# Attention and soft mixture of experts on one core: logits summed in PSUM, late scaling spread over three engines, full durations for the first loads, and the loop's buffers laid out by last use

## The chip, the core and the metric

One core of a Trainium2 chip runs the whole program. A core has five engines with a queue each: TensorE (PE; its weight loads are shown as PEld), VectorE (DVE), ScalarE (ACT), GpSimd (POOL) and SyncE (SP, which only issues transfers here). They run side by side and wait for each other by semaphores. The metric is the device time of one execution in microseconds (us), lower is better.

## The reference, cut to what matters

```python
scores = q @ k.T / 8                       # 8 batches x 8 heads, 576 tokens, head size 64
thresh = max(scores, -1) - tau             # keep only what is near the row's maximum
attn   = exp(where(scores >= thresh, scores, -1e9) - max(scores, -1))
attn  /= sum(attn, -1) + 1e-9
x      = (attn @ v), heads side by side    # [4608, 512]

logits = x @ phi                           # 32 slots
d      = softmax(logits, axis=0)           # over the 4608 tokens, one per slot
slots  = d.T @ x                           # [32, 512], 4 slots for each of 8 experts
slots  = relu(slots @ w1[e]) @ w2[e]       # 512 -> 1024 -> 512
out    = softmax(logits, axis=1) @ slots   # [4608, 512]
```

All of it is fp32. The dispatch weights `d` need a maximum over all tokens, so the kernel keeps a running maximum per batch and rescales what it has summed so far.

## The kernel before

The 64 heads are worked through as 32 pairs, `pair(p)`, four to a batch. A pair has nine row blocks of 128 queries (the ninth holds the 64 left of both heads). For each block PE multiplies q and k (L517, the ninth L522), DVE copies the scores out of PSUM with their maximum (L531, "max"), ACT takes the exponential (L544), POOL works out the threshold (L547), and DVE masks and sums the row (L551, "mask"). PE then transposes the result (L441 through the helper `ptr`), ACT copies it to SBUF (L446, `pTa`, `pTb`, `pTl`), and PE multiplies with v (L621). A further transpose, a scaling by the row sums on POOL (L636) and a transpose back (L641) give `x` and `xT`. In the last pair no later step can carry the row sums, so POOL scales the nine 128x576 blocks themselves (L565), with the reciprocals worked out on POOL (L558) and DVE (L561).

After each batch's fourth pair `dispatch(b)` runs, woven into the next pair: the logits of the batch as four products, one for each pair of heads, side by side in four column groups of PE (L700); a copy (ACT, L446, `l`); ten transposes (L712); a sum over the four products (DVE L717, L719); a copy for the left-over tokens (POOL L722); a transpose back (L441) and the maximum (DVE L732, L735); the factor `f` (ACT L737); a transpose of the maximum (`M`), the difference (DVE L744, L748) and its exponential (ACT L746, L750); and the weighted sums `csum` and `acc` (PE L770, L775; DVE L783). After the last batch `scale()` (L655 to L661) and `slot_in()` (L671, L674) make the slots' inputs `siT`, and the experts follow (L934 `h`, L968 `so`), then the combine. The combine's softmax (`csoft`, L805 to L815) is done in pieces by DVE and ACT.

**What sets the order.** `Order.plan` schedules the operations of the loop before the program is written: each has a duration, what it reads and writes, and a priority from `TABLE`; buffers are handed out as they come free. `Order.run` writes the program in the order of the planned starts. Every engine then works strictly in that order. PSUM is four regions, `ps0` to `ps3`. Where PE would idle at the start and at the end, transposes of the identity are put in (L433, "fillers"); 38 of them may stand behind the last AV product.

**Weights.** 46 of the 64 weight units (512 KB each) are loaded before the experts start: 26 into slots of their own (`w`), and 20 (`host`) into memory that the loop's buffers give back. Before, those buffers lie in five levels ordered by hand, and a host load waits until all levels that it lies in are done with. The 18 other units go into `w` slots as the experts' first layer frees them. All transfers are issued by SP in order.

Of the kernel before, what the change touches and what calls it, by code (L numbers as in the profile page):

```python
# [1108 lines left out]
```

## Time and profile before

| | us |
|---|---|
| median of 3 runs | 565.8 (565.67 to 566.19) |
| the profiled execution | 567.0 |
| its span, first to last instruction | 565.2 |
| PE busy | 536.4 (95%) |
| DVE busy | 476.1 (84%) |
| ACT busy | 458.2 (81%) |
| POOL busy | 257.9 (46%) |
| granted TensorE clock, mean | 0.985 of full |

Times in the rows below are counted from the span's start. A row of the timeline gives start, duration, engine, line, operation, what is written and read, how many instructions were joined, and in brackets the idle time ahead of it and what ended it. Instructions on one engine overlap by their pipelines, so the distance between starts, not the duration, is what one costs its engine.

### The profile page before, as it was taken

The page shows a single profiled execution, that of the slowest core. Times are in us where ns is not written, and L with a number is a line of the kernel's source. Part 1 is how long each engine was busy: PE and PEld are TensorE (multiplying, and loading weights), DVE is VectorE, ACT ScalarE, POOL GpSimd, SP SyncE. Part 2 cuts the span into 40 slices and gives each one's busy share as a digit, 9 for nine tenths or more (in the row PEclk, how much of TensorE's full clock was granted, in tenths as well). Part 3 has the DMA queues.
Part 4 walks back from the last instruction along what each step waited for, and adds up shares of the span by engine and source line. Part 5 has one row for each costly group of instructions (what it writes and reads, how often), then busy time and mean ns, then how long its engine had stood idle before and what let it go on. Part 6 is the DMA issues. An engine that isn't in the chain of part 4 may idle for free. (4 is left out here: it accounts for less than half of the span.)

```text
span 565.2 us, 17532 instructions
## 1 busy us (share of the span) xinstructions
PE 536.4 (95%) x6652; PEld 341.4 (60%) x6652; DVE 476.1 (84%) x1342; ACT 458.2 (81%) x784; POOL 257.9 (46%) x489
## 2 busy tenths in 40 slices
PE   8799999999999999999999999999999998899990
PEld 7566665666566666666666656666666565544470
DVE  5899998999999999998999899999999899322192
ACT  3699998999889999999899989998999889411171
POOL 1555553455345544554455545555555347311030
PEclk9799999999999999999999999999999999999996
DMA  7355555465446544432333333333333312899488
GB/s 170 70 160 164 163 161 154 121 188 177 102 127 178 167 132 140 102 94 52 81 88 89 88 89 87 88 89 87 89 87 88 88 63 54 319 404 409 194 357 313
DMA packets 31988, 82.99 MB, mean 147 GB/s; under 512 B 4640, under 2 KB 12832, under 8 KB 31904
## 3 DMA queue, kind: packets, MB, share of 16 engines
q1 hardware_dynamic: 31904, 81.87, 48.3%
q8 instruction: 53, 0.87, 0.7%
q14 instruction: 31, 0.25, 0.1%
HBM read 72.42 MB, written 9.44 MB: 145 GB/s over the span
## 5 line engine op out<-in xcount | busy, mean ns | idle before, releaser
L531 DVE TENSOR_SCALAR_CACHE_REDUCE ss<-ps 128x576 f32<-128x576 f32 x288 | 209.2, 749 | 23.4 <-ACT l L446 8.1
L547 POOL TENSOR_SCALAR thr<-nmx,pabs 128x1 f32<-128x1 f32 x288 | 130.0, 453 | 177.7 <-DVE ss L531 165.8
L551 DVE SCALAR_TENSOR_TENSOR p<-ss,thr,p 128x576 f32<-128x576 f32 x256 | 205.2, 823 | 3.8 <-POOL thr L547 2.7
L544 ACT ACTIVATE p<-ss,nmx 128x576 f32<-128x576 f32 x256 | 190.4, 781 | 13.0 <-DVE ss L531 13.0
L517 PE MATMUL ps<-k,q 64*128 64x288 f32 x1024 | 165.6, 430 | 3.9 <-POOL k L497 1.8
L441 PEld LDWEIGHTS ps<-ident,p 64*128 64x128 f32 x2304 | 92.9, 140 | 29.5 <-DVE p L551 7.0
L441 PE MATMUL ps<-ident,p 64*128 64x64 f32 x2304 | 105.2, 226 | 3.9 <-DVE ss L531 1.9
L517 PEld LDWEIGHTS ps<-k,q 64*128 64x128 f32 x1024 | 84.9, 190 | 36.1 <-ACT pTb L446 8.8
L446 ACT COPY pTb<-ps 128x1024 f32<-128x1024 f32 (+1 forms) x95 | 83.7, 881 | 2.6 <-PE ps L441 1.4
L621 PE MATMUL ps<-pTb,vv 128*64 128x320 f32 x512 | 76.0, 439 | 2.1 <-ACT pTa L446 1.8
L446 ACT COPY pTa<-ps 128x1024 f32<-128x1024 f32 x64 | 65.7, 1026 | 2.3 <-PE ps L441 2.1
L621 PE MATMUL ps<-pTa,vv 128*64 128x256 f32 x512 | 62.3, 385 | 1.5 <-DVE ss L531 0.8
L621 PEld LDWEIGHTS ps<-pTb,vv 128*64 128x64 f32 x512 | 34.1, 136 | 31.6 <-ACT pTa L446 3.1
L621 PEld LDWEIGHTS ps<-pTa,vv 128*64 128x64 f32 x512 | 33.9, 136 | 27.7 <-DVE ss L531 11.8
L621 PE MATMUL ps<-pTl,vv 128*64 128x256 f32 (+1 forms) x256 | 41.9, 406 | 0.0
L446 ACT COPY xT<-ps 128x256 f32<-128x256 f32 (+1 forms) x63 | 25.2, 400 | 13.5 <-PE ps L621 13.5
L446 ACT COPY pTl<-ps 128x256 f32<-128x256 f32 x64 | 23.8, 372 | 13.1 <-PE ps L441 12.3
L636 POOL TENSOR_TENSOR x<-x,ri 128x512 f32<-128x512 f32 x31 | 33.1, 1069 | 1.6 <-ACT x L446 1.5
L558 POOL TENSOR_SCALAR ri<-r 128x1 f32<-128x1 f32 (+1 forms) x36 | 20.0, 555 | 23.2 <-DVE pL L551 21.4
L565 POOL TENSOR_SCALAR pL<-pL,ri 128x576 f32<-128x576 f32 x32 | 26.5, 830 | 8.4 <-DVE ri L561 5.7
L899 POOL TENSOR_TENSOR c<-lall,crow 128x512 f32<-128x512 f32 x9 | 9.3, 1043 | 39.9 <-PE ct L433 39.9
L497 POOL TENSOR_SCALAR k<-k,flag 128x576 f32<-128x576 f32 x31 | 23.8, 769 | 7.0 <-DMA k<-in_kT 6.4
(134 smaller groups left out, 564.8 us busy)
## 6 DMA issues: line engine op xcount, KB each, us to landing
w<-in_w SPq DMA_DIRECT2D x44, 512.0 KB, 6.6
q<-in_qT SPq DMA_DIRECT2D x62, 288.0 KB, 4.3
vv<-in_vt SPq DMA_DIRECT2D x32, 320.0 KB, 4.0
host<-in_w SPq DMA_DIRECT2D x20, 512.0 KB, 6.4
k<-in_kT SPq DMA_DIRECT2D x62, 144.0 KB, 4.5
out<-w SPq DMA_DIRECT2D x8, 512.0 KB, 3.3
out<-host SPq DMA_DIRECT2D x8, 512.0 KB, 6.1
out<-host SPq DMA_DIRECT2D x4, 256.0 KB, 4.7
```

Of the source, the lines that this page charges most:

```text
L441: nc.tensor.transpose(out=s[:, g, c:c + 64], in_=ins[g], identity=ident[rows[g], rows[g]], tile_position=(64 * g, 0))
L446: G.add("ACT", 51 + 0.833 * n, nom, lambda: nc.scalar.copy(*io()), r, w)
L497: sc = lambda e, kc=kc: lambda: e.tensor_scalar(out=kt.t[:, kc], in0=kt.t[:, kc], scalar1=flag8, **one)
L517: nc.tensor.matmul(s.t[:, g, 0:HS], qt.t[rows[g], h, c * 128:(c + 1) * 128], kt.t[rows[g], h * HS:(h + 1) * HS], start=True, stop=True, ti ...
L531: dve(674, t + OFF['mx'], [s], [ss, nmx], lambda s=s, ss=ss, nmx=nmx: nc.vector.tensor_scalar(out=ss.t.rearrange("p (a k) -> p a k", a=2), ...
L544: G.add("ACT", 668 if away else 630, t + OFF['ex'], lambda sv=sv, nmx=nmx, view=view, away=away: nc.scalar.activation(view().rearrange("p ...
L547: pool(250, t + OFF['th'], lambda nmx=nmx, thr=thr, away=away: nc.gpsimd.tensor_scalar(out=thr.t, in0=nmx.t, scalar1=1.0 if away else -1.0 ...
L551: fn=lambda sv=sv, thr=thr, view=view, i=i, away=away: nc.vector.scalar_tensor_tensor(out=view().rearrange("p (a k) -> p a k", a=2), in0=sv(),
L558: pool(292, t + OFF['ri'], lambda e=e: nc.gpsimd.tensor_scalar(out=ri.t[:, e], in0=r.t[:, e], scalar1=1e-9, scalar2=1.0, op0=ALU.add, op1= ...
L565: pool(725, t + OFF['sc'], lambda k=k, view=view_: nc.gpsimd.tensor_scalar(out=view(), in0=view(), scalar1=ri.t[:, k:k + 1], **one), [ri[c ...
L621: nc.tensor.matmul(lone(w)[h * 64:(h + 1) * 64, 0:n], vv.t[:, v0:v0 + 64], p0, start=(kb == 0), stop=(kb == 4), tile_position=(0, h * 64), ...
L636: G.add("POOL", 1040, u + 6.8, own="new", r=[ri[0]], w=[x[j]], fn=lambda: nc.gpsimd.tensor_tensor(out=wide(), in0=wide(), in1=ri.t[:, 0:8] ...
```

## The change

1. **Logits.** The four products of a batch are summed in PSUM, in one tile of 192 columns: the 128-token chunk c goes to column group c (128 columns), the left-over tokens to 64 more columns. That is 32 products in place of 8. DVE takes the negated maximum straight from PSUM, ACT the exponential (`dT`) and a copy (`l4`), 192 columns each; two transposes of each and three copies give `d`, `lmain`, `lleft`. L712, L717, L719, L722, L744, L748 and the loop's transposes of `lall`, `ll` and `M` go. `xl` is now one batch's own with its upper half zero, so each batch adds its left-over tokens (two batches together before).
2. **Late scaling.** In the last pair, block 6 is scaled by DVE and block 7 by ACT, the other seven by POOL; both steps of the reciprocals are DVE's.
3. **First loads.** The planned durations of the transfers of the first three pairs are raised; the order table is new throughout. The order of loads on SP changes.
4. **Memory.** Each loop buffer has a pool of its own; they lie in the order of their planned last use, and a host load waits only for the buffers that it lies in and those released ahead of them.
5. The combine's DVE steps that stood in the last pair stand in the one before; `st4` is made later, on POOL; `siT` lies in the memory of `phi`.

```diff
-        -69.29, -40.08, -54.39, -166.86, 33.12, -19.81, -19.80, -168.20, -0.40, -236.51, -236.95, -153.88, 373.52, -143.51,
+        -281.55, -274.51, -289.04, -324.15, -256.85, -229.96, -223.08, -437.64, -189.50, -529.88, -365.53, -419.93, 528.97, -434.38,
...
+LATE_DVE = (6,)
+LATE_ACT = (7,)
...
-            G.add("SP", 1340, t0 - 18 + hs[0], keys, w=[kt[h] for h in hs])
+            G.add("SP", 1340 if p else 700, t0 - 18 + hs[0], keys, w=[kt[h] for h in hs])
...
-                G.add("SP", 620, t0 - 18 + hs[0], lambda g=g, a=hs[0], z=hs[-1] + 1: nc.sync.dma_start(
+                G.add("SP", (625 if p == 0 else 1250) if p < 3 else 800, t0 - 18 + hs[0], lambda g=g, a=hs[0], z=hs[-1] + 1: nc.sync.dma_start(
...
-        G.add("SP", 450, t0 - 12, lambda: nc.sync.dma_start(vv.t, vt[b, j]), w=[vv], after=vload[-1:])
+        G.add("SP", 1400 if p < 3 else 800, t0 - 12, lambda: nc.sync.dma_start(vv.t, vt[b, j]), w=[vv], after=vload[-1:])
...
+                    if k in LATE_DVE:
+                        dve(740, t + OFF['sc'], [ri[c]], [dst_], lambda f=f: f(nc.vector))
+                    elif k in LATE_ACT:
+                        G.add("ACT", 650, t + OFF['sc'], lambda k=k, view=view_: nc.scalar.activation(
+                            view(), view(), AF.Copy, scale=ri.t[:, k:k + 1]), [ri[c]], [dst_])
+                    else:
+                        pool(725, t + OFF['sc'], lambda f=f: f(nc.gpsimd), [ri[c]], [dst_])
...
+            for o, q in ((slice(0, 128), lambda c: slice(c * 128, c * 128 + 128)), (slice(128, 192), lambda c: slice(SM, S))):
                 for k in range(HP):
-                    nc.tensor.matmul(
-                        lone(w)[k * 32:(k + 1) * 32, 0:n], phi_sb[:, k, :], xT[k].t[:, q],
-                        start=True, stop=True, tile_position=(0, 32 * k))
...
+                    for c in range(4):
+                        nc.tensor.matmul(
+                            lone(wl)[c * 32:(c + 1) * 32, o], phi_sb[:, k, :], xT[k].t[:, q(c)], start=(k == 0),
+                            stop=(k == HP - 1), tile_position=(0, 32 * c), skip_group_check=True)
...
+        dve(269, u + 1.3, [wl], [M["own"]] if b else [new["run"]], lambda: nc.vector.tensor_reduce(
+            out=M.t[:, 0:1] if b else new.t[:, 1:2], in_=lone(wl)[:, 0:192], axis=AX.X, op=ALU.max, negate=True))
...
+        G.add("ACT", 250, u + 1.6, lambda: nc.scalar.activation(
+            dT.t, lone(wl)[:, 0:192], AF.Exp, bias=new.t[:, 1:2]), [wl, new["run"]], [dT])
...
-        dve(600, u + 3.3, [w], [lm[b]], lambda w=w: nc.vector.tensor_reduce(
-            out=lmain[b].rearrange("p c s -> p (c s)"), in_=view(w, slice(0, 128), slice(0, 128)), axis=AX.X, op=ALU.add))
...
+    end = lambda c: max(start[k] + G.ops[k][1] for k in users[c])
+    cells = sorted(((k, n) for k in shapes for n in range(SLOTS[k])), key=lambda c: -end(c) if c in users else 0)
...
+    for k, n in cells:
+        sides.append(tc.alloc_tile_pool(name=f"sb_{k}{n}", bufs=1, side="right", reuse_waits="tile"))
...
-        n = next(n for n in range(NL) if sum(x[1] for x in sides[:n + 1]) >= (i + 1) * 4096)
...
+        n = next(n for n in reversed(range(len(cells))) if sum(map(bytes_of, cells[n:])) >= (i + 1) * 4096)
```

On SP, the first loads. `k_181` and `k_312` are pair 0's keys, `q_182` and `q_316` its queries, `vv_183` and `vv_292` its values; `k_176`, `q_177`, `vv_143` and `k_268`, `q_272`, `vv_196` are pair 1's. Before:

```order
L490 DMA k_181<-in_kT 64x288 x2
L495 DMA q_182<-in_qT 64x576 x4
L819 DMA phi_sb<-in_phi 128x4x32
L502 DMA vv_183<-in_vt 128x640
L490 DMA k_181<-in_kT 64x288 x2
L495 DMA q_177<-in_qT 64x1152 x2
L502 DMA vv_143<-in_vt 128x640
L490 DMA k_176<-in_kT 64x2x288 x2
```

After:

```order
L475 DMA q_316<-in_qT 64x576
L470 DMA k_312<-in_kT 64x288 x2
L475 DMA q_316<-in_qT 64x576
L470 DMA k_312<-in_kT 64x288 x2
L475 DMA q_316<-in_qT 64x576 x2
L482 DMA vv_292<-in_vt 128x640
L470 DMA k_268<-in_kT 64x2x288 x2
L475 DMA q_272<-in_qT 64x1152 x2
L482 DMA vv_196<-in_vt 128x640
L786 DMA phi_sb<-in_phi 128x4x32
```

Pair 1's keys stand ahead of its queries, of its values and of `phi`, where they stood behind all three.

On PE, the last dispatch, from the logits to the sum `csum` of the weights (`l`, `lall`, `ll` logits, `M` the maximum, `dT`, `d`, `dl` the weights, `ident` alone a filler). Before:

```order
L700 MATMUL ps_215<-xT_127,phi_sb 32x320
L441 MATMUL ps_216<-ident,xT_129 128x64 x2
L441 MATMUL ps_216<-ident,xT_130 128x64 x2
L441 MATMUL ps_216<-ident,xT_126 128x64 x2
L441 MATMUL ps_216<-ident,xT_127 128x64 x2
L441 MATMUL ps_217<-ident,xT_127 128x64 x8
L433 MATMUL ps_218<-ident 128x128
L712 MATMUL ps_215<-ident,l_125 128x2x32 x10
L433 MATMUL ps_218<-ident 128x128 x10
L441 MATMUL ps_215<-ident,lall 128x64 x2
L441 MATMUL ps_215<-ident,ll_133 128x64 x2
L433 MATMUL ps_218<-ident 128x128 x8
```

After:

```order
L690 MATMUL ps_337<-xT_184,phi_sb 32x128 x4
L690 MATMUL ps_337<-xT_188,phi_sb 32x64 x4
L690 MATMUL ps_337<-xT_192,phi_sb 32x64 x4
L690 MATMUL ps_337<-xT_180,phi_sb 32x64 x4
L690 MATMUL ps_337<-xT_184,phi_sb 32x64 x4
L416 MATMUL ps_335<-ident 128x128 x5
L424 MATMUL ps_336<-ident,l_176 128x64 x4
L424 MATMUL ps_338<-ident,M_164 128x64 x2
L416 MATMUL ps_335<-ident 128x128 x4
L424 MATMUL ps_337<-ident,dT_168 128x64 x4
L416 MATMUL ps_335<-ident 128x128 x6
L737 MATMUL ps_336<-ones,d_160 32x1 x4
```

The logits are 32 small products now, the sixteen transposes of `xT` stand ahead of them (five rows like the ones at the top of before's list), and between logits and `csum` three groups of transposes are left, none of which waits for a sum on DVE.

On PE, the end of that dispatch up to the experts' first product. Before:

```order
L775 MATMUL ps_216<-xl_132,dl_139 32x128 x2
L655 MATMUL ps_218<-csum,msel 32x1 x4
L770 MATMUL ps_215<-x_131,d_134 32x256 x4
L775 MATMUL ps_215<-xl_132,dl_139 32x128 x2
L433 MATMUL ps_218<-ident 128x128 x6
L671 MATMUL ps_215<-stn,acc 128x32 x4
L433 MATMUL ps_218<-ident 128x128 x2
```

After:

```order
L737 MATMUL ps_336<-x_152,d_160 32x256 x4
L742 MATMUL ps_336<-xl_156,d_160 32x128 x2
L646 MATMUL ps_335<-csum,msel 32x1 x4
L416 MATMUL ps_335<-ident 128x128 x11
L662 MATMUL ps_336<-stn,acc 128x32 x4
L416 MATMUL ps_335<-ident 128x128 x12
```

The product of `csum` (L655, now L646) moves behind the whole of the weighted sum, and twelve fillers stand where two stood, between `slot_in`'s product and the experts' first.

On SP, the last loads of the loop: `vv` values, `host` weights. Before:

```order
L502 DMA vv_143<-in_vt 128x640
L423 DMA host_6893<-in_w 128x1024
L423 DMA host_6922<-in_w 128x1024
L423 DMA host_6947<-in_w 128x1024
L423 DMA host_6969<-in_w 128x1024
```

After:

```order
L406 DMA host_6909<-in_w 128x1024
L406 DMA host_6921<-in_w 128x1024
L482 DMA vv_196<-in_vt 128x640
L406 DMA host_7153<-in_w 128x1024
L406 DMA host_7177<-in_w 128x1024
```

Two host loads stand ahead of the last pair's values; the other eighteen behind, as before, each with waits of its own.

## Rows read from the trace of the kernel before

**Rows 1.** The page, part 1: busy time, share, instructions of each engine.

```profile
PE 536.4 (95%) x6652; PEld 341.4 (60%) x6652; DVE 476.1 (84%) x1342; ACT 458.2 (81%) x784; POOL 257.9 (46%) x489
```

**Rows 2.** Busy time by stretch: length, PE, PEld, DVE, ACT, POOL, PEclk, DMA share, GB/s.

```profile
20.00:24.00 4.00, 3.71 (x42) 3.18 (x44) 3.87 (x13) 3.60 (x6) 2.00 (x5) 0.50 0.12 25
```

**Rows 3.** Timeline of DVE: start, duration, instruction, [idle before].

```profile
7.39 0.76 DVE L531 TENSOR_SCALAR_CACHE_REDUCE ss<-ps 128x576 f32<-128x576 f32 x1 [1.96 <-PE ps L517]
...
10.42 0.37 DVE L497 TENSOR_SCALAR k<-k,flag 128x288 f32<-128x288 f32 x1 [0.23 <-DMA k<-in_kT]
...
17.31 0.82 DVE L551 SCALAR_TENSOR_TENSOR p<-ss,thr,p 128x576 f32<-128x576 f32 x1 [2.22 <-POOL thr L547]
...
21.57 0.75 DVE L531 TENSOR_SCALAR_CACHE_REDUCE ss<-ps 128x576 f32<-128x576 f32 x1
...
37.00 0.76 DVE L531 TENSOR_SCALAR_CACHE_REDUCE ss<-ps 128x576 f32<-128x576 f32 x1
```

**Rows 4.** Timeline of POOL, the same stretch.

```profile
16.29 0.74 POOL L497 TENSOR_SCALAR k<-k,flag 128x576 f32<-128x576 f32 x1 [5.74 <-DMA k<-in_kT]
```

**Rows 5.** Timeline of PE: the ninth block of pairs 2, 3, 27; one wait.

```profile
43.41 0.71 PE L522 MATMUL ps<-k,q 64*64 64x288 f32 x8
...
57.20 0.72 PE L522 MATMUL ps<-k,q 64*64 64x288 f32 x8
...
307.56 0.71 PE L517 MATMUL ps<-k,q 64*128 64x288 f32 x4
...
308.42 1.24 PE L517 MATMUL ps<-k,q 64*128 64x288 f32 x8 [0.15 <-ACT pTb L446]
...
410.39 0.71 PE L522 MATMUL ps<-k,q 64*64 64x288 f32 x8
```

**Rows 6.** Groups of instructions on PE by form, 59 to 470 us.

```profile
L770 PE MATMUL ps<-x,d 128*32 128x512 f32 x56 | 7.4, 603 | 0.0
...
L770 PE MATMUL ps<-ones,d 128*32 128x1 f32 x56 | 1.6, 170 | 0.0
```

**Rows 7.** Groups of instructions on DVE, the same stretch.

```profile
L717 DVE TENSOR_REDUCE lall<-ps 128x128 f32<-128x512 f32 x7 | 4.8, 692 | 0.2
```

**Rows 8.** Timeline of all engines around the last pair's end.

```profile
480.19 0.81 DVE L551 SCALAR_TENSOR_TENSOR pL<-ss,thr,pL 128x576 f32<-128x576 f32 x1
...
485.15 0.47 PE L641 MATMUL ps<-ident,x 64*128 64x64 f32 x8 [0.36 <-POOL x L636]
...
487.91 0.74 PE L621 MATMUL ps<-pTl,vv 128*64 128x320 f32 x4
```

**Rows 9.** Timeline of all engines, last dispatch to first weight product.

```profile
490.12 0.43 ACT L446 COPY l<-ps 128x320 f32<-128x320 f32 x1 [0.46 <-PE ps L700]
...
493.00 0.42 DVE L732 TENSOR_REDUCE M<-ps 128x1 f32<-128x256 f32 x1
...
495.44 0.24 PE L770 MATMUL ps<-ones,d 128*32 128x1 f32 x8
...
496.25 0.24 PE L655 MATMUL ps<-csum,msel 128*32 128x1 f32 x8
...
497.10 0.87 PE L433 MATMUL ps<-ident 128*128 128x128 f32 x6
...
497.84 1.05 PE L671 MATMUL ps<-stn,acc 128*128 128x32 f32 x8
...
498.73 0.42 PE L433 MATMUL ps<-ident 128*128 128x128 f32 x2
...
499.28 1.06 PE L934 MATMUL h<-w,siT 128*32 128x512 f32 x8
```

**Rows 10.** Waits of PE's weight loads, 499 to 534 us.

```profile
PEld h L934 <- DMA host<-in_w: 2.8, 4, 1.1
```

**Rows 11.** Timeline of SP, the last loads of weights.

```profile
492.33 5.43 SPq L421 DMA_DIRECT2D host<-in_w  x6
```

**Rows 12.** Busy time by stretch, while the weights are reloaded.

```profile
512.00:525.00 13.00, 13.00 (x116) 5.53 (x120) 3.27 (x5) 2.23 (x4) 2.04 (x2) 1.00 1.03 409
```

More of the change, by code (lines that the diff above doesn't have):

```diff
@@ L329, in softmax_attention_soft_moe @@
     )
-    st4 = cp.tile([128, 4, 32], F32, name="st4")
-    for g in range(4):
-        nc.vector.tensor_copy(st4[:, g, :], st1)
     ones = cp.tile([128, 1], F32, name="ones")
@@ new lines, in pair @@
+            if late and (i == 8 or h == 1):
+                e = slice(i // 2 * 2, i + 1)
+                dve(68, t + OFF['ri'], [r[k] for k in range(i // 2 * 2, i + 1)], [ri[c]], lambda e=e: nc.vector.tensor_scalar(
+                    out=ri.t[:, e], in0=r.t[:, e], scalar1=1e-9, scalar2=None, op0=ALU.add))
+                dve(75, t + OFF['ri'], [], [ri[c]], lambda e=e: nc.vector.reciprocal(ri.t[:, e], ri.t[:, e]))
+                for k in range(i // 2 * 2, i + 1):
+                    dst_, view_ = (pL, lambda: pL.t) if i == 8 else (
+                        p2s[c][k % 2], lambda c=c, k=k: p2s[c].t[:, k % 2 * S:(k % 2 + 1) * S])
+                    f = lambda e, k=k, view=view_: e.tensor_scalar(
+                        out=view(), in0=view(), scalar1=ri.t[:, k:k + 1], **one)
+                    if k in LATE_DVE:
[5 more added lines that the diff above has]
+                        pool(725, t + OFF['sc'], lambda f=f: f(nc.gpsimd), [ri[c]], [dst_])
+            elif i == 8:
@@ L726, in dispatch @@
-        w = Buf("s")
-        ptr(1 + odd, u + 4, [lm[b]] + [ll4] * odd, [w], lambda w=w: [
-            (w.t, 0, [lmain[b][a].rearrange("p c s -> p (c s)") for a in rows])] + [
-            (w.t, 64, [ll4.t[a].rearrange("p c s -> p (c s)") for a in rows])] * odd)
-        new = batch_state(b + 1)["M"]
-        dve(202 + 130 * odd, u + 4.2, [w], [M["own"]] if b else [new["run"]], lambda w=w: nc.vector.tensor_reduce(
-            out=M.t[:, 0:1] if b else new.t[:, 1:2], in_=w.t[:, :, 0:64 * (1 + odd)], axis=AX.XY, op=ALU.max))
@@ L734, in dispatch @@
-        if b > 0:
-            dve(69, u + 4.3, [M], [new["run"]], lambda: nc.vector.tensor_reduce(
-                out=new.t[:, 1:2], in_=M.t, axis=AX.X, op=ALU.max))
-            G.add("ACT", 190, u + 4.5, lambda: nc.scalar.activation(
-                f.t, new.t[:, 1:2], AF.Exp, bias=M.t[:, 1:2], scale=-1.0), [M["run"], new["run"]], [f])
-        w = Buf("s")
-        ptr(1, u + 5, [new["run"]], [w], lambda w=w: [
-            (w.t, 0, [new.t[a, 1:2].to_broadcast([64, 128]) for a in rows])])
@@ new lines, in dispatch @@
+        G.add("PE", 1313, u + 1, logits, xT + [ph], [wl], mode=COLS4)
+        new = batch_state(b + 1)["M"]
+        dve(269, u + 1.3, [wl], [M["own"]] if b else [new["run"]], lambda: nc.vector.tensor_reduce(
+            out=M.t[:, 0:1] if b else new.t[:, 1:2], in_=lone(wl)[:, 0:192], axis=AX.X, op=ALU.max, negate=True))
+        if b > 0:
+            dve(69, u + 1.4, [M], [new["run"]], lambda: nc.vector.tensor_reduce(
+                out=new.t[:, 1:2], in_=M.t, axis=AX.X, op=ALU.min))
+            G.add("ACT", 200, u + 1.5, lambda: nc.scalar.activation(
+                f.t, M.t[:, 1:2], AF.Exp, bias=new.t[:, 1:2], scale=-1.0), [M["run"], new["run"]], [f])
@@ L751, in dispatch @@
+        w = Buf("s")
+        ptr(2, u + 2.5, [l4], [w], lambda w=w: both(w, l4))
+        act_copy(128, u + 2.8, [w], [lm[b]], lambda w=w: (
+            lmain[b].rearrange("p (g c) s -> p g (c s)", g=2), w.t[:, :, 0:64]))
+        dve(102, u + 2.9, [w], [ll[b]], lambda w=w: nc.vector.tensor_copy(lleft[pl, b // 2], w.t[rows[1], 0, 64:64 + NS]))
         if b == B - 1:
+            w = Buf("s")
+            ptr(1, u + 5, [new["run"]], [w], lambda w=w: [
+                (w.t, 0, [new.t[a, 1:2].to_broadcast([64, 128]) for a in rows])])
@@ L784, in weigh @@
                     out=dst, in0=dst, scalar=f.t, in1=lone(w)[:, 0:n], op0=ALU.mult, op1=ALU.add))
[L786 removed]
+        weigh(0, 1, 1, lambda c: ones, lambda c: (slice(0, 1), ones_left), csum, cs, 200, u + 6)
         pieces = 2 if b == B - 1 else 1
@@ L887, in softmax_attention_soft_moe @@
     ps_t = ctx.enter_context(tc.tile_pool(name="ps_t", bufs=3, space=PSUM, reuse_waits="tile"))
+    st4 = tl.tile([128, 4, 32], F32, name="st4")
+    for g in range(4):
+        nc.gpsimd.tensor_copy(st4[:, g, :], st1)
     mask = tl.tile([128, E // 4, 4, 32], F32, name="mask")
```

176 lines of the change are left out of this document (67 added, 109 removed), and 43 rows, old and new, of the table TABLE.

## The prediction

> **What bounds the kernel now.** I read the page's busy times first, then the stretches, then the timelines. PE is busy 95% of the span and DVE 84% [rows 1], but what a change is worth depends on the stage. In the loop PE sets the pace: pair 2's ninth block starts at 43.41 and pair 3's at 57.20, so a plain pair costs 13.79 us; 24 pairs, six batches, lie between 57.20 and 410.39, 58.87 us a batch [rows 5]. Four plain pairs would be 55.16, so a dispatch costs some 3.7. At both ends PE waits for others. At the start DVE loses 2.22 us at 17.31 for a threshold [rows 3], which POOL could not make because it stood 5.74 us in front of pair 1's keys and began to scale them at 16.29 [rows 4]; after this hole the granted clock is 0.50, the lower of the two levels, through 20 to 24 us [rows 2]. At the end the last dispatch is a chain of small steps from 488.65 (last AV product, 487.91 and its 0.74) to 499.28 [rows 8, 9], and then PE's weight loads wait 2.8 us, four times, for host loads [rows 10].
>
> **The first loads.** The order of SP puts 2432 KB up to and with pair 1's keys before (k 288, q 576, phi 64, vv 320, q 576, vv 320, k 288) and 1472 KB after. At before's mean rate from the span's start, 2432 KB by 16.29 [rows 4], they land near 16.29 x 1472/2432 = 9.9 us, an estimate; pair 1's queries, 576 KB more, near 13.7. POOL's three thresholds that stand ahead of the scaling are done by then. So the wait at 17.31 goes, and what is late next is DVE itself. From its first max (7.39) to pair 1's first max (21.57) there are 14.18 us [rows 3]: 9 max, 7 mask, the second half of the keys' scaling, and waits of 0.23 and 2.22. After has the same 9 and 7, with the scaling ahead of the first max: that may start 0.2 later, since it now waits for the second keys, sixth in the queue. 14.18 - 2.45 - 0.3 + 0.2 = 11.6, so pair 1's first max stands at 19.0 instead of 21.57, **-2.6 us**. A second gain hangs on the clock. From pair 1's first max to pair 2's ninth block there are 43.41 - 21.57 = 21.84 us, from pair 2's (37.00) to pair 3's ninth block 57.20 - 37.00 = 20.20 [rows 3, 5]: pair 1 paid 1.64 more, with the clock at 0.50 in it. The hole ahead of the fall, PE without work while DVE waits, closes; I take the fall as gone, **-1.6**, and keep zero as the other end.
>
> **The dispatches in the loop.** On PE a pass costs about (603 - 170)/511 = 0.85 ns a column, and a product has two passes [rows 6]. Before: 256 and 320 columns, four products side by side, 2 x 576 x 0.85 = 0.98 us. After: four products follow each other in each column group, 4 x 2 x (128 + 64) x 0.85 = 1.30, **0.3 more**. Ten transposes of `l` (half of them side by side), those of `lall`, `ll`, `M` go, eight of `dT` and `l4` come: some 0.2 less. `xl` is weighed in every batch instead of every second, 0.2 more in the even ones. Together +0.1 each, and no longer wait for it: seven dispatches **+0.7**, with 0 and +2 as ends. On DVE L717 (0.69) [rows 7] and three smaller steps go and a copy comes, about 1 us less per dispatch, 0.25 less on POOL. They lie beside PE's work, so I take nothing for them. Plain pairs keep their operations, PE's changes of mode among them (six a pair in either order); only the order differs.
>
> The page "TensorE: Matmul & The Clock Gate" of the Trainium skill, section "Wait — 56ns, not 53.3ns?", says that matmuls start at least about 25 ns apart however small they are. By that the 64-column passes, four to a step, would take 100 ns instead of 54, eight steps +0.37 us a dispatch, 2.6 in the loop, and the sum below would be -3.9 in place of -6.5. The trace speaks against it where column groups differ: eight one-column products take 0.24 in all with 170 ns for one [rows 6, 9], so their starts lie about 10 ns apart.
>
> **The last pair.** DVE sets its end. Dispatch 7's relief (1 us), the combine's steps moved one pair up and less strain from POOL stand against block 6's scaling (one DVE pass over 576 columns, about a max's distance, 0.7) and five additions for the reciprocals. POOL, which PE still waits for at 485.15 [rows 8], has two scalings of about 0.74 less; ACT has one more, in a stretch where it waits for PE. I take **-0.2** at the last AV product, ±1.
>
> **The last dispatch.** Before, the last logits are copied at 490.12 and the maximum starts at 493.00 [rows 9]; between them a copy, ten transposes, two sums, a copy and two transposes, with a hand-over each. After, the maximum reads PSUM at once: -2.9, but the logits take 0.3 longer and the transposes of `xT` stand ahead of them (sixteen, 0.7): maximum at 491.1. From maximum to `csum` 2.44 becomes about 2.2 (exponential, transposes, copy instead of transposes, difference, exponential). So `csum` comes 2.1 earlier. Then a part is given back. L655 stood 0.81 behind `csum`'s product; after, it stands behind the other half of the weighing too, 497.10 - 496.25 = 0.85 less its own 0.08, +0.77. From `slot_in`'s product (497.84) to the experts' first (499.28) it was 1.44, of which 0.89 to the first filler. A filler costs (0.87 - 0.42)/4 = 0.11, and twelve stand there now: 0.89 + 12 x 0.11 = 2.2, +0.77. The step ends **-0.6**; without the fillers it would be -1.3.
>
> **Host loads.** By the order of after I looked up which step ends the last buffer that each host load needs and gave it before's time for that step (D = 481.0, the last mask [rows 8]; A = 488.65). Two loads go ahead of the last values, the third can start at D - 3.8, the ninth at D + 1.1, the thirteenth at D + 5.2, the last at A + 3.5. Before, the last six were issued between 492.33 and 497.76 [rows 11], that is up to A + 9.1. At 409 GB/s, which the reloads reach [rows 12], a load takes 1.28 us, so from here on the queue of loads is the limit, and counting back from the issue times the twentieth lands near A + 13.5. PE begins the experts at A + 10.0 (10.6 less 0.6) with its 26 own units, two passes of 512 columns each, four side by side, 26 x 2 x 512 x 0.85/4000 = 5.7 us: it asks for the first host unit at A + 15.7. The waits [rows 10] go, **-2.2** (of the 2.8, 0.6 lay beside products under way). Reloads follow the release of slots by PE and end earlier too.
>
> **Sum.** -2.6 - 1.6 + 0.7 - 0.2 - 0.6 - 2.2 = -6.5. The profiled execution took 567.0 (span 565.2, 1.8 around it), 1.2 above the median: 560.5 by it, **559.3** by the median.
>
> **Rivals.**
> - *The clock falls all the same*, because PE still waits for DVE between 14 and 18 us: the 1.6 stays lost, 560.9. For: PE has little work until pair 1. Against: the hole is 2 us shorter. 0.2.
> - *The host loads do not come earlier*, since one early-released neighbour that is in truth read late holds a whole row of them, or the queue's one order does: -2.2 is not had, 561.5. The change does not do there what it says. 0.1.
> - *The relief of DVE and POOL shortens the loop after all*, since PE waits in the dispatches: half of the 1 us in seven, -3.5: 555.8. Against: PE's waits in the loop are short and few. 0.1.
> - *Slower: the new order has PE wait in each pair.* At 308.42 PE stood for a copy on ACT (`pTb`); four passes at 307.56 were followed 0.86 later, where 2 x 288 x 0.85 = 0.49 would do [rows 5], so one such wait costs 0.38. If the new table, repeated in each pair, has it once a pair, 31 x 0.38 = +11.8: 571. From 0.21 a pair it eats the whole gain. Before's plain pairs are regular, so its table has none; the new one puts every step elsewhere. 0.1.
>
> **How the numbers follow.** The forecast has 0.5, its own range 557 to 562 by the ends above. The range leaves out the slower rival and half of the loop's: 554.3 to 563.8. This kernel's measurement tells 0.2%, 1.1 us, from no change; slower 0.1, within it 0.06 (losses in the pairs that just eat the gain), faster 0.84.
>
> **What would show it.** Start: no POOL idle of several us ahead of L477, pair 1's first max near 19, the clock full at 20 to 24 us, pair 2's ninth block near 39.2. Loop: 58.9 to 59.0 a batch. End: maximum about 2.5 behind the last AV product, `csum` 4.7, the experts' first product 10.0, no wait of `h` for `host`. I am wrong if the plain pair is not 13.8, if PE waits for ACT in each, or if host loads land behind their use.

## The result and the profile after

The changed kernel takes 568.75 us, median of 11 runs (567.49 to 571.53), against 566.3 of the kernel before, measured beside it. The ratio is 1.0041, interval 1.0024 to 1.0058: slower by 0.4%, where 559.3 was forecast. The profiled execution took 567.5 (span 565.7), one of the shortest of the 11. One run of experiment e7, at 1291 us, counts as slow and is left out of that experiment's ratio.

The stages are best compared by the starts of the ninth block of a pair (timeline of PE, kernel after; pair 2's, those on both sides of the second dispatch, pair 30's and pair 31's with the last AV product):

```profile
38.30 0.72 PE L502 MATMUL ps<-k,q 64*64 64x288 f32 x8
```

```profile
137.64 0.72 PE L502 MATMUL ps<-k,q 64*64 64x288 f32 x8
...
157.07 0.72 PE L502 MATMUL ps<-k,q 64*64 64x288 f32 x8
```

```profile
456.58 0.72 PE L502 MATMUL ps<-k,q 64*64 64x288 f32 x8
...
477.56 0.71 PE L502 MATMUL ps<-k,q 64*64 64x288 f32 x8
...
490.58 0.70 PE L612 MATMUL ps<-pTl,vv 128*64 128x320 f32 x4
```

| stretch, by the ninth blocks | before | after | difference |
|---|---|---|---|
| start to pair 2 | 43.41 | 38.30 | -5.1 |
| 21 plain pairs from pair 2 to pair 30, each | 13.70 | 13.56 | -2.9 in all |
| 7 pairs with a dispatch, sum | 124.4 | 133.5 | +9.1 |
| pair 30 to pair 31 | 21.94 | 20.98 | -1.0 |
| pair 31 to the end of the last AV product | 11.18 | 13.72 | +2.5 |
| from there to the experts' first product | 10.63 | 11.35 | +0.7 |
| from there to the end | 65.92 | 63.07 | -2.9 |

The sum is +0.5, the difference of the spans. The start, the plain pairs, the stretch from pair 30 to pair 31 and the experts gained 11.9 us; the dispatches in the loop, the end of the last pair and the last dispatch gave back 12.3. The medians lie 2.45 apart, more than the spans, because the profiled execution of before is 0.7 above its median and this one 1.2 below.

**The start** is as forecast. POOL scales pair 1's keys at 11.02 with 0.63 of idle time in front (5.74 in [rows 4]), DVE has no hole, and pair 1's first max, the tenth max, starts at 18.70 (21.57 in [rows 3]). The clock stays full (0.50 in [rows 2]). Timelines of POOL and DVE, and the busy times by stretch (length, PE, PEld, DVE, ACT, POOL, PEclk, DMA share, GB/s):

```profile
11.02 0.74 POOL L477 TENSOR_SCALAR k<-k,flag 128x576 f32<-128x576 f32 x1 [0.63 <-DMA k<-in_kT]
```

```profile
18.70 0.76 DVE L509 TENSOR_SCALAR_CACHE_REDUCE ss<-ps 128x576 f32<-128x576 f32 x1
```

```profile
20.00:24.00 4.00, 4.00 (x50) 2.53 (x48) 4.00 (x13) 3.79 (x7) 2.95 (x7) 1.00 0.01 3
```

**The dispatches.** The first one takes 17.68 us as before (17.62); the next five 19.4 to 19.5, where before had 18.1 and 17.5 in turn; the seventh 18.6 (17.6). Timeline of PE, kernel before, the ninth blocks on both sides of the second dispatch:

```profile
143.40 0.72 PE L522 MATMUL ps<-k,q 64*64 64x288 f32 x8
...
161.48 0.72 PE L522 MATMUL ps<-k,q 64*64 64x288 f32 x8
```

In the kernel after, the waits of ACT, DVE and PE between 60 and 455 us (us in total, times, longest) have these lines, of which before has no counterpart for the first and the third; DVE waited for ACT's copy of `l` there too, 8.1 us in seven dispatches, but with a maximum of the scores (L531), not of the logits:

```profile
ACT dT L702 <- PE ps L612: 15.6, 6, 2.6
```

```profile
DVE M L695 <- ACT l L429: 10.1, 7, 1.5
```

```profile
PE ps L497 <- ACT xT L429: 4.9, 6, 0.9
```

In the pair that carries the second dispatch (timeline of all engines, from 137.64 to 157.07) they form a chain. DVE stands idle for 1.46 us ahead of its maximum of the logits, first for the logits and then for ACT's copy of them; the exponential `dT` could follow the second maximum (149.16, 0.15 long) but waits until an AV product, L612 at 150.42, is done; behind `dT` stand ACT's exponentials and copies for the running pair, and PE runs dry:

```profile
147.46 0.32 ACT L429 COPY l<-ps 128x192 f32<-128x192 f32 x1
147.81 0.36 DVE L695 TENSOR_REDUCE M<-ps 128x1 f32<-128x192 f32 x1 [1.46 <-ACT l L429]
...
149.16 0.15 DVE L698 TENSOR_REDUCE M<-M 128x1 f32<-128x2 f32 x1
...
150.42 0.60 PE L612 MATMUL ps<-pTl,vv 128*64 128x256 f32 x4
...
151.07 0.42 ACT L702 ACTIVATE dT<-ps,M 128x192 f32<-128x192 f32 x1 [2.59 <-PE ps L612]
...
151.55 0.34 PE L424 MATMUL ps<-ident,dT 64*128 64x64 f32 x4 [0.52 <-ACT dT L702]
...
153.31 0.76 PE L497 MATMUL ps<-k,q 64*128 64x288 f32 x4 [0.93 <-ACT xT L429]
```

Where the order lists what each writes, the reason can be read: the logits lie in the first half of PSUM region `ps1`, and the AV product that waits its turn while DVE works on the maximum is written into the second half of the same region. The plan counts the halves as two buffers; the program that comes out guards the region as one, so `dT`, placed behind that AV product, waits for it. In the first dispatch there is no second maximum, `dT` stands ahead of the AV product, and nothing waits.

**The end.** No product of the experts waits for a host load any more ([rows 10] had 2.8 us): the time from the experts' first product to the first transpose of their result is 10.44 us, 12.53 before. But the last pair is longer. Timeline of all engines:

```profile
480.20 1.01 ACT L429 COPY pTa<-ps 128x1024 f32<-128x1024 f32 x1
...
481.26 0.92 PEld L424 LDWEIGHTS ps<-ident,p 64*128 64x128 f32 x20 [1.61 <-ACT pTa L429]
...
482.03 1.05 DVE L532 TENSOR_SCALAR ri<-r 128x2 f32<-128x2 f32 x2
...
483.26 0.78 ACT L543 ACTIVATE p<-p,ri 128x576 f32<-128x576 f32 x1 [1.02 <-DVE ri L534]
...
483.94 0.99 ACT L429 COPY pTa<-ps 128x1024 f32<-128x1024 f32 x1
...
485.63 0.29 PEld L612 LDWEIGHTS ps<-pTa,vv 128*64 128x64 f32 x4
```

```profile
478.00:482.00 4.00, 1.72 (x40) 1.20 (x34) 3.42 (x9) 3.35 (x6) 3.83 (x7) 1.00 0.73 263
482.00:486.00 4.00, 2.94 (x52) 2.47 (x48) 2.04 (x8) 2.98 (x5) 2.01 (x2) 0.68 0.98 305
```

PE's weight loads wait 1.61 us for a copy that stands behind two exponentials on ACT; the second copy of `pTa` (483.94) stands behind ACT's new scaling of block 7 (L543), which waits 1.02 for the reciprocals. DVE makes these late: while POOL scales `x`, the first of its two additions (L532) takes 0.99 us, where the second takes 0.14. PE is busy 1.72 of 4 us, the granted clock falls to 0.68 behind that, and sixteen AV products take 2.53 (1.95 is usual). All AV products of both halves stand behind this. The last dispatch then reads:

```profile
494.64 0.36 DVE L695 TENSOR_REDUCE M<-ps 128x1 f32<-128x192 f32 x1 [2.74 <-ACT l L429]
...
497.10 0.16 PEld L737 LDWEIGHTS ps<-ones,d 128*32 128x32 f32 x8 [0.17 <-issue]
...
500.25 0.98 PE L662 MATMUL ps<-stn,acc 128*128 128x32 f32 x8
...
502.63 0.16 PEld L914 LDWEIGHTS h<-w,phi_sb 128*32 128x32 f32 x8 [0.30 <-PE ps L416]
```

The maximum comes 3.36 behind the last AV product (4.35 before), `csum` 5.82 (6.79), and the experts' first product 11.35 (10.63): `slot_in`'s product to the experts' first takes 2.38 where it took 1.44.

### The profile page after: what moved, and what is told of

It is laid out like the page before. It is cut to its first block, busy times and chain, and to the rows that moved or that the text cites. A ratio compares the mean times of both kernels' runs of the same rounds, so it can differ in the third digit from the quotient of the medians.

```text
span 565.7 us, 18326 instructions
## 1 busy us (share of the span) xinstructions
PE 535.9 (95%) x7022; PEld 346.4 (61%) x7022; DVE 468.8 (83%) x1327; ACT 458.0 (81%) x789; POOL 251.6 (44%) x478
## 4 chain that ended last, share of the span: by engine, by line
PE 71%; ACT 17%; DVE 5%; issue 4%; SPq 1%; DMA 0%; DVEq 0%; POOL 0%; ACTq 0%; POOLq 0%
PE ps L612 25%; PE ps L497 19%; PE ps L424 14%; ACT p L519 6%; ACT pTa L429 3%; PE h L914 2%; PE ps L502 2%; ACT pTb L429 2%; PE so L948 2%; PE ps L632 1%; PE ps L737 1%; DVE ss L509 1%; ACT xT L429 1%; DVE cT L906 1%; ACT pL L519 1%
## 5 line engine op out<-in xcount | busy, mean ns | idle before, releaser
L509 DVE TENSOR_SCALAR_CACHE_REDUCE ss<-ps 128x576 f32<-128x576 f32 x288 | 208.0, 754 | 12.5 <-ACT pTl L429 8.9
L522 POOL TENSOR_SCALAR thr<-nmx,pabs 128x1 f32<-128x1 f32 x288 | 120.5, 419 | 199.7 <-DVE ss L509 190.1
L525 DVE SCALAR_TENSOR_TENSOR p<-ss,thr,p 128x576 f32<-128x576 f32 x256 | 201.4, 811 | 9.5 <-ACT p L519 9.0
L519 ACT ACTIVATE p<-ss,nmx 128x576 f32<-128x576 f32 x256 | 186.5, 778 | 18.9 <-DVE ss L509 18.7
L424 PE MATMUL ps<-ident,p 64*128 64x64 f32 x2304 | 100.8, 225 | 2.8 <-ACT pTa L429 1.5
L424 PEld LDWEIGHTS ps<-ident,p 64*128 64x128 f32 x2304 | 87.5, 140 | 19.1 <-ACT pTa L429 6.4
L429 ACT COPY pTb<-ps 128x1024 f32<-128x1024 f32 (+1 forms) x95 | 79.9, 872 | 2.3 <-PE ps L424 1.5
L612 PE MATMUL ps<-pTb,vv 128*64 128x320 f32 x512 | 75.9, 438 | 0.1
L612 PE MATMUL ps<-pTa,vv 128*64 128x256 f32 x512 | 62.9, 388 | 0.0
L612 PEld LDWEIGHTS ps<-pTb,vv 128*64 128x64 f32 x512 | 34.0, 136 | 36.0 <-issue 10.0
L612 PEld LDWEIGHTS ps<-pTa,vv 128*64 128x64 f32 x512 | 34.2, 138 | 26.1 <-DVE ss L509 9.0
L556 POOL TENSOR_SCALAR pL<-pL,ri 128x576 f32<-128x576 f32 x31 | 34.9, 1126 | 27.7 <-DVE ri L552 25.6
L612 PE MATMUL ps<-pTl,vv 128*64 128x256 f32 (+1 forms) x256 | 41.9, 406 | 0.0
L525 DVE SCALAR_TENSOR_TENSOR pL<-ss,thr,pL 128x576 f32<-128x576 f32 x32 | 26.5, 828 | 0.0
L612 PEld LDWEIGHTS ps<-pTl,vv 128*64 128x64 f32 x256 | 18.4, 137 | 12.7
```

The source lines that it names most:

```text
L424: nc.tensor.transpose(out=s[:, g, c:c + 64], in_=ins[g], identity=ident[rows[g], rows[g]], tile_position=(64 * g, 0))
L429: G.add("ACT", 51 + 0.833 * n, nom, lambda: nc.scalar.copy(*io()), r, w)
L509: dve(674, t + OFF['mx'], [s], [ss, nmx], lambda s=s, ss=ss, nmx=nmx: nc.vector.tensor_scalar(out=ss.t.rearrange("p (a k) -> p a k", a=2), ...
L519: G.add("ACT", 668, t + OFF['ex'], lambda sv=sv, nmx=nmx, view=view: nc.scalar.activation(view().rearrange("p (a k) -> p a k", a=2), sv(), ...
L522: pool(250, t + OFF['th'], lambda nmx=nmx, thr=thr: nc.gpsimd.tensor_scalar(out=thr.t, in0=nmx.t, scalar1=1.0, scalar2=pabs, op0=ALU.mult, ...
L525: fn=lambda sv=sv, thr=thr, view=view, i=i: nc.vector.scalar_tensor_tensor(out=view().rearrange("p (a k) -> p a k", a=2), in0=sv(), scalar ...
```

## The experiments

Each is one edit, to the changed kernel, to the kernel before or to the first experiment (e1); e11 and e12 join two edits, on e1 and on e5. The order is planned anew for each. Ratios are to the kernel before, measured beside it (its medians 566.6 to 567.1).

**e1: `dT` from SBUF.**

```diff
-            dT.t, lone(wl)[:, 0:192], AF.Exp, bias=new.t[:, 1:2]), [wl, new["run"]], [dT])
+            dT.t, l4.t, AF.Exp, bias=new.t[:, 1:2]), [wl, l4, new["run"]], [dT])
```

The copy `l4` is also entered ahead of `dT`, each with the priority that it had. The traces of the changed kernel and of e1 list the same instructions in the same order on PE, DVE, ACT and POOL; only the operand of `dT` differs.

> The changed kernel with one edit: the exponential dT reads the logits' copy l4 in SBUF instead of the PSUM tile; every engine's order of work stays the same. Theory A (dT waits, in six of seven loop dispatches, for the AV product that is written into the other half of its PSUM tile, 2.6 us of ACT each, and this makes the dispatch pair 19.43 us instead of 17.7): the idle time ahead of dT falls from 15.6 us to under 2, dispatch pairs 2 to 7 take 17.6 to 17.9, the time falls by 6 x 1.7 = 10 us to some 558.5 (ratio to the kernel before 0.986). Rival B (what delays the dispatch is DVE's maximum, which waits 1.46 us for ACT's copy of the logits): this wait stays, dispatch pairs stay at 19.4, ratio 1.00. Rival C (the 32 small products cost PE the time): also 19.4 and 1.00.

560.78 us (four runs, 560.08 to 561.46), ratio 0.9891 (0.9873 to 0.9909): 8 us below the changed kernel by one operand. Waits of ACT and DVE as above, and the ninth blocks around the same dispatch:

```profile
ACT dT L705 <- DVE M L698: 5.2, 6, 0.9
```

```profile
DVE M L695 <- ACT l L429: 10.1, 7, 1.5
```

```profile
138.01 0.72 PE L502 MATMUL ps<-k,q 64*64 64x288 f32 x8
...
156.05 0.72 PE L502 MATMUL ps<-k,q 64*64 64x288 f32 x8
```

The wait for the AV product is gone (15.6 us before this edit), the dispatch pairs two to six are 17.9 to 18.1, and DVE's wait for the copy is as long as it was, 10.1 us. That is theory A; B and C would have left 19.4. The expected 17.7 came 0.3 short. The seven dispatch pairs sum to 126.3 us, 133.5 in the changed kernel: 7.3 of the 9.1 that they had lost. The seventh keeps its 18.6.

**e5: the maximum ahead of the copy.** On e1, the copy `l4` is made to depend on the maximum.

```diff
-        act_copy(192, u + 1.7, [wl], [l4], lambda: (l4.t, lone(wl)[:, 0:192]))
+        act_copy(192, u + 1.7, [wl, M["own"] if b else new["run"]], [l4], lambda: (l4.t, lone(wl)[:, 0:192]))
```

> The kernel of e1 (dT from SBUF) with the copy of the logits planned behind DVE's maximum, so that the maximum need not wait for the copy (1.46 us of DVE in each dispatch of e1). Theory A (in e1 PE no longer waits in the loop, so what DVE loses there costs nothing): dispatch pairs stay at 17.9 to 18.1, time within 1 us of e1 (560.8). Rival B (DVE's late maximum still sets the dispatch): dispatch pairs fall to 17.0 or less, 6 to 8 us below e1.

560.36 us, ratio 0.9896 (0.9882 to 0.9911), the same as e1. But not for theory A's reason: all seven dispatch pairs take 17.2 to 17.6, and pair 31's ninth block stands at 465.55 instead of 470.30. Of DVE's 10.1 us ahead of the maximum 5.7 are left, now for the logits themselves; the wait for the copy did cost some 0.7 in each dispatch. The gain of 4.7 us was lost whole in the last pair, where POOL makes four scalings in a row and the clock is 0.50 through 470 to 478:

```profile
465.55 0.21 PEld L502 LDWEIGHTS ps<-k,q 64*64 64x64 f32 x8 [0.39 <-ACT x L429]
...
468.78 3.90 POOL L538 TENSOR_SCALAR p<-p,ri 128x576 f32<-128x576 f32 x4
...
471.29 1.04 PEld L424 LDWEIGHTS ps<-ident,p 64*128 64x128 f32 x18 [2.25 <-POOL p L538]
```

**e2: all late scalings on POOL.**

```diff
-LATE_DVE = (6,)
-LATE_ACT = (7,)
+LATE_DVE = ()
+LATE_ACT = ()
```

> The changed kernel with the late scaling undone: all nine blocks of the last pair on POOL, the reciprocals still on DVE. Theory (the spread itself costs the end: block 6's pass stands on DVE between the last mask and the AV products, and ACT's copies wait for block 7): the last AV product, at 491.28 and 2.6 us later than in the kernel before, comes 1 to 2 us earlier, time -1 to -2. Rival (the new order is at fault: both halves of the last AV products, 256 and 320 columns, stand behind all scalings, whoever makes them): the last AV product comes 0.5 to 1.5 us later still, since POOL has two more blocks of 0.74 us; time +0.5 to +1.5.

570.03 us, ratio 1.0075 (1.0045 to 1.0104), some 1.3 above the changed kernel. From the ninth block to the end of the last AV product 16.0 us, 13.7 in the changed kernel. So the theory falls: without the spread the end is longer, and by more than the rival said. How much of that is the spread is open, since the plan also moved the AV products of `pTa` ahead of the last transposes, and the clock is 0.50 at 486 to 490. This trace also shows the clock fall in the dispatches: two of them take 20.84, and the granted clock is 0.70 and 0.59 behind the stretch in which PE waits:

```profile
149.00:153.00 4.00, 3.03 (x40) 1.85 (x37) 2.26 (x9) 1.76 (x4) 0.53 (x2) 1.00 0.38 147
153.00:158.60 5.60, 5.12 (x64) 3.33 (x64) 3.88 (x11) 3.44 (x9) 0.26 (x1) 0.70 0.02 3
```

The runs of the changed kernel lie between 567.5 and 571.5 with mean clocks of 0.990 down to 0.979; those of e1, where PE no longer waits in the dispatch, lie within 1.4 us. That the scatter is this fall fits, and was not tried by itself.

**e8: block 7 on DVE.** On e1.

```diff
-LATE_DVE = (6,)
-LATE_ACT = (7,)
+LATE_DVE = (6, 7)
+LATE_ACT = ()
```

> The kernel of e1 with block 7 of the last pair scaled by DVE, not ACT. In the changed kernel ACT's scaling of block 7 waits 1.02 us for the reciprocal, and the copy of the second half of pTa, ready by 482.3, stands behind it until 483.94. Theory (this copy is what the last AV products wait for): from the last pair's ninth block to the last AV product's end 13.7 us become some 12.4, time -1.3 against e1. Rival (the order of the transposes, both halves behind the last scalings, is at fault): 13.7 stays or grows by DVE's 0.5.

562.22 us, ratio 0.9928 (0.9913 to 0.9943), 1.4 above e1. The copy came 1.1 earlier, as the theory wanted, and the whole did not gain: the AV products of `pTa` start right behind it at 476.64 (478.36 in e1), at half clock, and take 3.68, and the plan has put the transposes of the second half behind them:

```profile
475.57 1.01 ACT L429 COPY pTa<-ps 128x1024 f32<-128x1024 f32 x1 [0.44 <-PE ps L424]
...
476.64 0.29 PEld L612 LDWEIGHTS ps<-pTa,vv 128*64 128x64 f32 x4 [0.18 <-ACT pTa L429]
```

From the ninth block to the end of the last AV product it is 15.8 us, 14.3 in e1. An earlier copy alone does not shorten the end; what it would give with PE's old order was not tried.

**e9: the old priorities for the last pair.** On e1, the list "last" of the order table as in the kernel before.

```diff
     ("last", [
-        758.77, 747.51, 747.50, 201.79, 762.75, 242.12, 283.37, 138.94, 136.41, 324.27, 233.08, 318.47, 62.44, 128.49,
+        402.04, 385.23, 376.30, 542.46, 380.79, 430.35, 176.51, -264.49, 527.76, 129.31, 486.76, -124.82, -243.97, 390.32,
...
```

> The kernel of e1 with the old priorities for the last pair's steps (the new ones everywhere else). Theory (the new order of the last pair costs the 2.6 us by which the last AV product comes later): the first half's AV products stand ahead of the last scalings again, from the ninth block to the last AV product 11.2 to 12 us, time -2 against e1. Rival (the old priorities do not fit the new ones around them): PE waits earlier in the pair, no gain or a loss.

568.32 us, ratio 1.0025 (1.0009 to 1.0041): the rival. PE waits 1.81 and 2.37 us for DVE's steps and 0.97 and 2.17 for ACT's copies, and from the ninth block to the last AV product 20.5 us pass. The old list does not fit the new ones around it.

**e10: fillers in the last pair.** On e1, twenty transposes of the identity that may stand wherever PE is planned idle behind the ninth block.

```diff
+    mid = Buf("w")
+    ninth = max(k for k, o in enumerate(G.ops) if k >= recent[-1] and o[0] == "PE" and o[5] == QUADS)
+    G.scope("load", NP * N9 + 900)
+    for i in range(20):
+        G.add("PE", 109, NP * N9 + 900, lambda i=i: tr(mid.t[:, i % 4 * 128:i % 4 * 128 + 128], ident),
+              [], [mid], after=[ninth] if i == 0 else [], mode=WHOLE)
```

> The kernel of e1 with twenty fillers in the last pair, at the places where PE is planned idle behind the ninth block (19 of them ahead of the transposes that wait at 471.8 and 474.0 in e1). In e1 PE is busy 1.73 of 4 us at 470 to 474, the granted clock is 0.50 in the 4 us behind that, and the sixteen AV products of pTa take 3.08 us, where 1.95 is usual. Theory (the fall of the clock is a part of what the end loses): the clock stays at 1.00 through 474 to 482, these products take 1.95, the last AV product comes 1.5 us earlier in relation to the ninth block, time -1.5 against e1. Rival (the end is set by the chain over DVE, POOL and ACT, and slower products are hidden behind ACT's copies): the clock stays full and the last AV product moves by less than 0.5.

558.92 us (558.81 to 559.18), ratio 0.9861 (0.9839 to 0.9883), 1.9 below e1. Apart from the fillers the traces of e1 and e10 list the same instructions in the same order on every engine. The clock stays full, the products take 1.95, and from the ninth block to the last AV product it is 12.5 us, 14.3 in e1. Busy time by stretch of e1, then of e10, and PE's row of e10:

```profile
470.00:474.00 4.00, 1.73 (x37) 1.05 (x34) 3.41 (x11) 3.74 (x5) 3.82 (x6) 0.98 0.64 181
474.00:478.00 4.00, 3.62 (x54) 3.15 (x56) 2.51 (x7) 2.38 (x4) 2.74 (x3) 0.50 0.98 291
```

```profile
470.00:474.00 4.00, 3.92 (x49) 2.96 (x45) 3.41 (x9) 3.67 (x5) 3.83 (x7) 1.00 0.78 228
474.00:478.00 4.00, 3.21 (x65) 2.57 (x67) 2.64 (x8) 2.65 (x5) 2.47 (x2) 1.00 0.97 294
```

```profile
477.49 1.95 PE L612 MATMUL ps<-pTa,vv 128*64 128x256 f32 x16
```

Work that nobody needs, put where PE waits, made the kernel faster; the fall of the clock was the larger part of what the end had lost, 1.7 of 3.1 us. The 1.4 us left against before's 11.2 stay open: e2, e8 and e9 made the end longer, and each of them changed PE's order in the last pair as well.

**e7: fewer fillers behind the last dispatch.** On e1.

```diff
-WARM = 38
+WARM = 26
```

> The kernel of e1 with 26 fillers behind the last AV product instead of 38, so that none is left between slot_in's product and the experts' first; nothing else changes. Theory (the fillers hold PE's queue for longer than the wait that they should fill): from slot_in's product to the experts' first 1.44 us instead of 2.38, time -0.9 against e1. Rival (the wait of PE lets the granted clock fall in the experts' first layer): the same 1.44, and the clock below 1.00 in the 10 us behind it, time 0 or worse.

559.98 us by the median of all four runs, 0.8 below e1; ratio 0.9889 (0.9867 to 0.991), not told apart from e1's by its interval. The rows do tell: `slot_in`'s product stands at 493.62, the experts' first at 494.97, 1.35 behind it instead of 2.38, and it now waits for `siT` (which lies in `phi_sb`) and not for the fillers in PE's queue; the clock stays at 1.00 through 494 to 509, so the rival does not hold:

```profile
493.62 0.98 PE L662 MATMUL ps<-stn,acc 128*128 128x32 f32 x8
494.97 1.50 PE L917 MATMUL h<-w,phi_sb 128*32 128x512 f32 x12 [0.38 <-DVE phi_sb L665]
```

**e11: e7 and e10 together.**

> e1 with the twenty fillers in the last pair and without the twelve behind slot_in's product: e7 and e10 together, the version meant to beat both kernels. If their gains are independent, 0.9 + 1.5 below e1, 558.4 by its median of 560.8, ratio 0.985; if one of them works only by the clock of the other, 559.5.

558.22 us (557.77 to 558.57), ratio 0.9848 (0.9825 to 0.9871): 2.6 below e1, and this beats both kernels, by 1.5% and, by the two ratios, 1.9%. The interval overlaps e10's; the rows show that both gains are there, 12.5 us from the ninth block to the last AV product and 10.3 from there to the experts' first product (11.3 in e1).

**e12: the same on e5.**

> e5 (the maximum ahead of the logits' copy: dispatch pairs of 17.2 to 17.4 us, pair 31's ninth block 4.7 us earlier than in e1, all of it lost again in the last pair at half clock) with the same two edits on the fillers. Theory (the half clock is the larger part of that loss): the last AV product comes 2.5 us earlier than in e5, time 556.5 to 557.5. Rival (the order of the last pair is: POOL makes four scalings of 0.97 us in a row from 468.8 on, with the thresholds behind them): at most 1 us, 559.

559.64 us, ratio 0.9869 (0.9846 to 0.9891): the rival. POOL's scalings in a row still let PE run dry; the clock is 0.89 in 470 to 474 and 0.50 in 474 to 478. The 4.7 us of the faster loop are there (pair 31's ninth block at 466.13, 470.77 in e11), and the last pair loses more than that: from its ninth block to the last AV product 18.9 us, 12.5 in e11, and the whole is 1.4 above e11.

**e3: the memory order alone, on the kernel before.** The lines on `cells`, `sides` and `users` of the change, with `TABLE` and all else as before.

```diff
-        n = next(n for n in range(NL) if sum(x[1] for x in sides[:n + 1]) >= (i + 1) * 4096)
+        n = next(n for n in reversed(range(len(cells))) if sum(map(bytes_of, cells[n:])) >= (i + 1) * 4096)
```

> The kernel before with part 4 alone: the loop's buffers in the order of their planned last use, a host load waiting only for what it lies in. The order of work stays the same but for one load on SP. Theory: the waits of PE's weight loads for host (2.8 us, four) go, the experts' first layer is 2.2 us shorter, everything ahead of it unchanged: ratio 0.996. Rival (the earlier transfers collide with the last pairs' loads, or the reloads behind them become the wait): waits for w appear in place of those for host, ratio 0.999 to 1.001.

563.53 us, ratio 0.995 (0.9927 to 0.9973). No wait for `host` is left among PE's weight loads, and from the experts' first product to the end of the span it takes 64.0, 65.9 before; pair 31's ninth block to that product is unchanged, 21.8. So part 4 is worth 1.9 us by itself. The median fell by more; in the profiled execution the clock did not fall at 20 to 24 us, which the edit does not touch, and pair 2's ninth block stands at 41.33 (43.41 before).

**e4: the first loads' durations alone, on the kernel before.**

```diff
-            G.add("SP", 1340, t0 - 18 + hs[0], keys, w=[kt[h] for h in hs])
+            G.add("SP", 1340 if p else 700, t0 - 18 + hs[0], keys, w=[kt[h] for h in hs])
...
-        G.add("SP", 450, t0 - 12, lambda: nc.sync.dma_start(vv.t, vt[b, j]), w=[vv], after=vload[-1:])
+        G.add("SP", 1400 if p < 3 else 800, t0 - 12, lambda: nc.sync.dma_start(vv.t, vt[b, j]), w=[vv], after=vload[-1:])
```

> The kernel before with part 3's durations alone and the old order table. Its planned order differs from before's in more places than the first pairs, so the front is what to read. Theory (the hole at 17.31 comes from pair 1's keys standing behind values and phi): POOL scales pair 1's keys before 12 us, pair 1's first max comes near 19 instead of 21.57, the clock stays full at 20 to 24 us, pair 2's ninth block near 39 instead of 43.41. Rival (the new table, not the order of loads, closes the hole): the keys come early and the first max still comes after 20. The whole time: -4 if the old table still fits the loop; the old table was made with the old durations, so it may lose that again.

567.45 us, ratio 1.0008 (0.9996 to 1.0019), no difference. The front reads against both theories: the loads came in the old order, pair 1's keys last, and POOL scaled them at 16.20, as late as before; yet DVE had no hole, pair 1's first max stood at 19.57 and the clock stayed full. The plan, told of the late landing, had put two more thresholds ahead of the scaling:

```profile
14.12 0.69 POOL L547 TENSOR_SCALAR thr<-nmx,pabs 128x1 f32<-128x1 f32 x1 [3.80 <-DVE ss L531]
15.53 0.69 POOL L547 TENSOR_SCALAR thr<-nmx,pabs 128x1 f32<-128x1 f32 x1 [0.72 <-DVE ss L531]
16.20 0.73 POOL L497 TENSOR_SCALAR k<-k,flag 128x576 f32<-128x576 f32 x1
```

```profile
19.57 0.74 DVE L531 TENSOR_SCALAR_CACHE_REDUCE ss<-ps 128x576 f32<-128x576 f32 x1
```

Pair 2's ninth block came 3.1 earlier (40.27), and the old table lost 2.7 of it in the next pair (16.47 instead of 13.79).

## Why the prediction was wrong

- **First loads: right in the hole, open in the clock.** -4.2 was forecast, -5.1 measured, of which -2.9 up to pair 1's first max (-2.6 forecast). The cause was named too narrowly: what stood behind POOL's scaling in its queue mattered, not only when the keys landed (e4). That the other 2.2 are the change's is not shown: e3 has before's loads and before's wait for the keys (POOL idle 4.38 us), and in its profiled execution the clock stayed at 1.00 all the same. Part of this term may be the luck of the executions that were profiled.
- **Plain pairs: not forecast.** "Before's plain pairs are regular, so its table has none" was wrong, and the rows read for it held the answer. The 0.38 us that I priced as a rare wait [rows 5] stood in before's plain pairs: in one of them, twelve products of q and k take 2.09 us, in the changed kernel's 1.68. PE counts as busy in both; the row of its weight loads shows the wait, for the same copy `pTb`. Between 60 and 455 us thirteen such groups of before are longer by this 0.4, none of the changed kernel. The gain is -0.14 a pair over 21 (13.55 against 13.79 in two of each three, 13.43 in both kernels in the one behind a dispatch). Timelines of PE and of its weight loads, a plain pair of before, then PE of after:

```profile
293.77 2.09 PE L517 MATMUL ps<-k,q 64*128 64x288 f32 x12
```

```profile
294.62 0.79 PEld L517 LDWEIGHTS ps<-k,q 64*128 64x128 f32 x8 [0.60 <-ACT pTb L446]
```

```profile
297.46 1.68 PE L497 MATMUL ps<-k,q 64*128 64x288 f32 x12
```

- **Loop dispatches: the step that failed.** "+0.7, with 0 and +2 as ends" was +9.1. The work on PE was sized well enough: the 32 products stand 1.46 us from first to next (1.30 forecast with no step between), and the starts within a step lie 7 ns apart, so the other price weighed in the prediction, 100 ns a step, did not come about: a step costs 56 to 109 ns by its columns. What failed is "and no longer wait for it" and "they lie beside PE's work, so I take nothing for them". I costed the new readers of PSUM by their durations and never asked what they wait for. The order showed `ps1` as the source of `dT` and, two rows of PE ahead of it in time, `ps1` as the AV product's target. It was there to be read before the run; e1 shows that this one wait cost 7.3 us of the 9.1. The maximum's wait for the copy covers the rest and more: with both out (e5) the seven dispatches sum to 121.6 us, 2.9 less than before. That is near the -3.5 of the rival in which the relief of DVE and POOL shortens the loop; which of the steps that went gives it was not tried.
- The maximum's wait for the copy of the logits is of the same kind: two engines read one bank. The Trainium skill, page "PSUM — Partial Sum Buffer", section "PSUM bank collisions raise a hardware error", says to guard PSUM by bank and quadrant, reads by two engines included. The runs agree that the program does so: the maximum starts only behind ACT's copy, 1.46 us of waiting in a dispatch and 10.1 in all, and with the maximum put first (e5) 5.7 of them are left. The wait of `dT` goes beyond that rule, since the two halves are two banks.
- **Last pair: wrong**, -0.2 ± 1 forecast, -1.0 to its ninth block and +2.5 behind it. I counted what DVE and POOL gain and lose and took PE's waits from before; in the new order PE has done its other work by 478 and stands still, and the clock falls. e10 gives back 1.7 of it by fillers alone, against e1.
- **Last dispatch: wrong by 1.3.** The part given back was forecast (0.77 and 0.77, measured 0.75 over two steps and 0.94). The gain up to `csum` was 1.0, not 2.1: the maximum waits for the copy here too, and the transposes of `xT` wait for a copy of their own that I had left out.
- **Host loads: right**, -2.2 forecast, -2.1 measured (12.53 to 10.44 us), and the same 10.44 by this part alone (e3).
- The rival on the slower side named a wait in each pair, with the right engine (PE behind ACT) and the wrong place; by its point of decision, 0.21 us a pair, the dispatches' loss of 9.1 is 0.29 a pair.
- The ends of the range, 554.3 and 563.8, are choices: no sum of the prediction gives them.
